# Dilated sliding-window attention, then a two-layer product: the first loads of w_in by columns, later landings in the order's list, longer zero matmuls, and new ranks

## The chip, the cores and the metric

The kernel runs on one core of a Trainium2 chip. The metric is the device time of one execution in microseconds. Before the change it is 316.99 us, the median of 4 runs (316.38 to 318.28).

## The reference

Attention of 8 batches with 8 heads, 576 positions and head size 64, under two masks: heads 0 to 3 see the last 32 positions, heads 4 to 7 every fourth of the last 128. Its output, with heads side by side, is the input x (4608 x 512) of two products with a leaky ReLU between them.

```python
scores = scale * np.matmul(q, k.transpose(0, 1, 3, 2))
mask_plain = (rel >= 0) & (rel < window)                                  # window = 32
mask_dil = (rel >= 0) & (rel < window * dilation) & (rel % dilation == 0)  # dilation = 4
attn = softmax(where(mask, scores, -1e9))
x = (attn @ v), transposed to (4608, 512)
h = x @ w_in                       # w_in is 512 x 2048
g = np.maximum(0.01 * h, h)
out = g @ w_out                    # w_out is 2048 x 512, all float32
```

## The kernel before

**Work.** Four pairs of batches make four blocks `m` of 1152 token columns, each cut into three chunks of 384. For a chunk, `up` (L776) makes 16 groups `j`, each of four matmuls that add up over the four 128-row blocks of w_in and give 128 of the 2048 hidden columns (the "products with w_in", L784); ACT applies the leaky ReLU (L791) into `gt`. `down` (L815) then makes three token tiles `tt`, each of four pieces `p` of four matmuls with w_out (the "products with w_out", L829); piece p needs the rows of w_out for j = 4p to 4p+3. DVE copies the sums out (L839) and SP stores them. The weights stay in SBUF in 16 bits.

**Attention.** `attend` (L878) goes through the head pairs in the order 2, 3, 0, 1: `load_group` loads q, k and v, `turn` transposes q and k (for the first two batches on TensorE, L555, with copies out of PSUM at L505 and L507), and `unit` (L636) makes scores (L664 adds the mask's bias for some batches, L667 and L683 the scores), exp on ACT (L689), a mask multiply on DVE (L703) where no bias was added, the products with v and with ones (L715 to L747), and the reciprocal of the sum as ln and exp on ACT (L759, L761). A multiply on DVE (L765) puts the normalized result into `xt`. The first two batches are done in two parts: part 0 covers positions below 384 or so and feeds chunks 0 and 1; part 1, the rest, feeds chunk 2 with data of its own (`load_rest`, L388).

**Loading the weights.** `load_w` (L419) loads w_in in eight eighths and w_out in eight, 512 KB each, into buffers that are still free, and casts each in two halves of 512 elements a partition. An eighth of w_in holds 512 columns of two of the four row blocks, so groups 0 to 3 need both eighths 0 and 1:

```python
            j0, i0 = n // 2 * 512, n % 2 * 2
            src = dram(moe_w_in, i0 * 128 * DFF + j0, [DFF, 128], [128 * DFF, 2], [1, 512])
            dst = [w_in[:, i * DFF + j0:i * DFF + j0 + 512] for i in (i0, i0 + 1)]
```

The casts of eighths 0 and 1, and those of w_out, go to POOL or DVE; those of eighths 2 to 7 of w_in to POOL alone.

**Order.** Nothing is scheduled by the compiler: every instruction is a task with an engine, a cost, dependencies and a rank, and `_Plan.run` (L83) makes one list. It goes forward in its own time and takes, on each engine, the ready task of the lowest rank. The engines then run their parts of that list strictly in order, whatever really becomes ready first. The plan estimates a load's landing from its issue, a shared server with a service time by packet size (`took`, L228), and an amount `LATE` that is added for loads after the opening; the loads of the opening get 0. The string `FIRST` (L19) gives the opening's loads their ranks from -1499 upwards: b and v are batch 0's q, k and v, i an eighth of w_in, o one of w_out, c and y batch 1's q, k and v, 0 and 1 the rests. `CON` is the rank of the load of the masks.

The ranks of compute tasks: chunk c's group j has `begins[c] + j * 1.3` (chunk 0 from 0, chunk 1 from 20.8), its product piece with w_out `begins[c + 1] + (tt * 4 + p) * 1.73 + 0.6`. The head pairs of batches 0 and 1 have `first + step * n` from `RANKS` (L20), in the order batch 0 part 0, batch 0 part 1, batch 1 part 0, batch 1 part 1; later batches have theirs from `WHEN`.

**Zero matmuls.** Where the plan leaves TensorE a gap ahead of the first product with w_out, the last loop fills it with matmuls of zeros (L919), 256 columns each, one for each 0.2 us of the gap (0.14 near the start).

Of the kernel before, what the change touches and what calls it, by code (L numbers as in the profile page):

```python
# [15 lines left out]
AHEAD, LATE = 5.0, 4.0  # L16
WHEN = (-5.0, 15.0, 50.0, 77.0, 112.0, 138.0, 172.0, 200.0)
CON = -1484.5
FIRST = "bvbviiii0iicooiicoyoooooy1"  # L19
RANKS = ((20.0, 6.0), (-40.0, 2.0), (20.0, 1.0), (40.0, 3.0))  # L20


def _constants():
# [36 lines left out]
class _Plan:  # L60
# [5 lines left out]
    def add(self, eng, dur, lat, deps, fn, prio, soft=0.0, kind=""):  # L66
        choices = eng if isinstance(eng, tuple) else ((eng, dur),)
        t = _Task(choices, lat, deps, fn, prio, soft, len(self.tasks), kind)
        self.tasks.append(t)
        return t  # L70
# [66 lines left out]
def kernel(  # L137
# [10 lines left out]
    nc = tc.nc  # L148
# [6 lines left out]
    DFF = moe_w_in.shape[1]  # L155
# [14 lines left out]
    def sbuf(name, shape, dt=FP16):  # L170
        return sb.tile(shape, dt, name=name)

    def bank(name, dt=FP32):
        return ps.tile([128, 512 if dt == FP32 else 1024], dt, name=name)

    def at(tl, p0, p1, off, *dims):

        row = tl.ap[0][0]
        return bass.AP(tensor=tl.tensor, offset=tl.offset + p0 * row + off,
                       ap=[[row, p1 - p0]] + [list(d) for d in dims])  # L180

    def dram(t, off, *dims):
        return bass.AP(tensor=t.tensor, offset=t.offset + off, ap=[list(d) for d in dims])
# [6 lines left out]
    w_in = sbuf("w_in", [128, NI * DFF])  # L190
# [21 lines left out]
    warm = sbuf("warm", [128, 512])  # L212
# [7 lines left out]
    fps = [bank(f"fps{i}") for i in range(2)]  # L220
# [7 lines left out]
    def took(n, size):  # L228
        for a, ta, b, tb in ((4, 9.0, 128, 15.0), (128, 15.0, 256, 19.0), (256, 19.0, 1024, 48.0),
                             (1024, 48.0, 2048, 85.0)):  # L230
            if size <= b:
                return n * (ta + (tb - ta) * (size - a) / (b - a)) / 16e3
        return n * size / 23.5 / 16e3

    def load(queue, dst, src, n, size, deps, prio):
        eng = ENG[queue]
        return plan.dma(queue, 0.7 if size == 128 else 0.48, took(n, size), deps,
                        lambda e: eng.dma_start(dst, src), prio,  # L238
                        LATE if prio > -1500 + len(FIRST) else 0.0)

    def cast(dst, src, n, deps, prio, engines=("POOL",)):
        cost = {"POOL": 0.05 + n * 0.00102, "DVE": 0.08 + n * 0.00056, "ACT": 0.06 + n * 0.00087}

        def fn(e):
            if e == "ACT":
                nc.scalar.copy(out=dst, in_=src)
            else:
                ENG[e].tensor_copy(out=dst, in_=src)  # L248
        return add(tuple((e, cost[e]) for e in engines), None, 0.2, deps, fn, prio, 0.0, "cast")
# [6 lines left out]
    def ring(name, n, users):  # L256
# [5 lines left out]

    t_warm = clear("POOL", warm.bitcast(FP32), 0.25, 0.0, -2000)
    t_id = load("ACT", con[:, 0:128], const_d[:, 0:128], 128, 256, [], -1498.95)
    t_bias = load("ACT", con[:, 128:128 + NMASK], const_d[:, 128:128 + NMASK], 128, 2 * NMASK, [],
                  -1498.5)
    t_con = load("SP", con[:, 128 + NMASK:NCON], const_d[:, 128 + NMASK:NCON], 128, 2 * NMASK, [],
                 CON)

# [13 lines left out]
    def clear_ones(slots, deps, prio=-700):  # L283
        for i in slots:
            t_ones["d", i] = clear("POOL", at(vd[i].bitcast(FP32), 0, 128, D // 2, [64, 16], [1, D // 2]),
                                   0.48, TWO_ONES, prio,
                                   deps)
            t_ones["p", i] = clear("POOL", at(vp[i].bitcast(FP32), 0, 128, D // 2, [64, 12], [1, D // 2]),
                                   0.38, TWO_ONES, prio,
                                   deps)  # L290
# [6 lines left out]
    CENG = ("POOL", "DVE")  # L297
# [121 lines left out]
    def load_w(n, prio):  # L419

        home, off, prev = w_home[n]
        f = home if home.dtype == FP32 else home.bitcast(FP32)
        st = f[:, off:off + 1024]
        users = w_used[n]
        old = w_used[prev] if prev is not None else []
        if n < 8:
            j0, i0 = n // 2 * 512, n % 2 * 2
            src = dram(moe_w_in, i0 * 128 * DFF + j0, [DFF, 128], [128 * DFF, 2], [1, 512])
            dst = [w_in[:, i * DFF + j0:i * DFF + j0 + 512] for i in (i0, i0 + 1)]
        else:  # L430
            j0 = 2 * (n - 8)
            src = dram(moe_w_out, j0 * 128 * DM, [DM, 128], [128 * DM, 2], [1, DM])
            dst = [w_out[:, j * DM:j * DM + DM] for j in (j0, j0 + 1)]
        t = load("SP", at(st, 0, 128, 0, [512, 2], [1, 512]), src, 256, 2048, old, prio)
        for i in range(2):
            c = cast(dst[i], st[:, i * 512:i * 512 + 512], 512, [t], prio, ("POOL",) if 2 <= n < 8 else CENG)
            users.append(c)
            if n < 8:
                for j in range(n // 2 * 4, n // 2 * 4 + 4):
                    w_in_t.setdefault(j, []).append(c)  # L440
            else:
                w_out_t[j0 + i] = [c]
# [417 lines left out]
    ranks = {}  # L860
    for n, step in enumerate(FIRST):
        seen = FIRST[:n].count(step)
        if step in "io":
            load_w(seen + (8 if step == "o" else 0), tick())
        elif step in "bvcy":
            ranks["bvcy".index(step) // 2, 1 - seen, step in "vy"] = tick()
        else:
            ranks[int(step)] = tick()
# [9 lines left out]
    def attend(b, part, first, step):  # L878
        units = {None: (0, 1, 2), 0: (0, 1), 1: (2,)}[part]
        if part == 1:  # L880
            load_rest(b, ranks[b])
        for n, hp in enumerate((2, 3, 0, 1)):
            if part != 1 and n % 2 == 0:
                load_group(b, hp // 2, *(ranks[b, hp // 2, i] if b < EARLY else tick()
                                         for i in (0, 1)))
            got = turn(b, hp, part or 0, first + step * n)
            for u in units:
                unit(b, hp, part or 0, u, got, first + step * n)

    n_c = 0  # L890
    for m in range(B // 2):
        for b in (2 * m, 2 * m + 1):
            if b < EARLY:
                attend(b, 0, *RANKS[2 * b])
                if b == 0:
                    release()
                    clear_slots(range(4, NT), -700, x_done[0, 0][-1:])
                    clear_ones((2,), x_done[0, 0][-1:])
                attend(b, 1, *RANKS[2 * b + 1])
            else:  # L900
# [14 lines left out]
    order = plan.run()  # L915


    def idle(e):
        nc.tensor.matmul(fps[0][:, 0:256], warm[:, 0:128], warm[:, 0:256], start=True, stop=True)  # L919

    pe = [t for t in order if t.eng == "PE"]
    for t, u in zip(pe, pe[1:]):
        if u.kind == "D":
            break
        x = t.start + t.dur + 0.1
        step = 0.14 if t.start < 8 else 0.2
        while t.start > 0.5 and x + step + 0.1 < u.start:
            w = _Task((("PE", step),), 0.0, [], idle, 0, 0.0, 0, "w")
            w.eng, w.start, w.dur, w.done = "PE", x, step, x + step
            order.append(w)  # L930
            x += step
# [37 lines left out]
```

## Time and profile before

| | |
|---|---|
| median of 4 runs | 316.99 us (316.38 to 318.28) |
| profiled execution | 317.19 us |
| its span, first to last instruction | 315.4 us |
| mean granted TensorE clock | 0.993 |
| TensorE busy | 303.0 us, 96% of the span |
| HBM read, written | 41.30 MB, 9.44 MB |
| PE waits for DVE (xt) before the second w_in product | 2.2 us, once |
| PE waits for ACT (exp) before L664 | 1.4 us, twice |
| the chain that ended last | 85% PE, 4% DVE, 4% DMA |

Durations come from one execution taken by the hardware profiler; times are microseconds from the span's start. PE is the matmul part of TensorE and PEld its weight loads, which overlap. Matmuls are pipelined, so a row's length includes a tail that the next row overlaps. A bracket at the end of a row says how long the engine stood idle before it and what ended the wait. POOL is GpSimd, DVE VectorE, ACT ScalarE, SP the engine that issues most of the DMAs. The page cuts the span into 40 slices of 7.9 us and gives each engine's busy share in tenths.

### The profile page before, as it was taken

What the parts mean: (1) busy time and instruction counts of PE and PEld (TensorE: products, weight loads), DVE (VectorE), ACT (ScalarE), POOL (GpSimd) and SP (SyncE); (2) the same over time, 40 slices, a digit from 0 to 9 for tenths busy, and PEclk for the clock granted to TensorE, in tenths of its full rate; (3) what the DMA queues carried; (4) which work ended last, traced back from release to release, by engine and by line L of the source; (5) the groups of instructions that cost most, each with busy time, mean ns of one, the idle gap of its engine ahead of it and who ended that gap; (6) DMA issues with size and microseconds to landing.
All of it is one profiled execution on the core that took longest, in us unless ns stands there. A gap on an engine that the chain in (4) does not pass through costs nothing.

```text
span 315.4 us, 6335 instructions
## 1 busy us (share of the span) xinstructions
PE 303.0 (96%) x2261; PEld 180.4 (57%) x2261; DVE 174.4 (55%) x394; ACT 219.8 (70%) x501; POOL 120.1 (38%) x176
## 2 busy tenths in 40 slices
PE   7869889999999999999999999999999999999995
PEld 3536545557776565666665555555555555555544
DVE  5845993725886978877659766664443421000011
ACT  3846773767889999999989888788787743334310
POOL 4458655365472755737447555370000000000000
PEclk9989999999999999999999999999999999999999
DMA  7999998999999999999989988711111111211113
GB/s 246 297 328 395 392 346 157 212 199 222 188 191 197 164 239 235 171 245 194 169 221 172 184 206 167 172 35 33 35 33 35 33 34 41 56 39 35 34 33 100
DMA packets 160223, 51.14 MB, mean 162 GB/s; under 512 B 139200, under 2 KB 151616, under 8 KB 160192
## 3 DMA queue, kind: packets, MB, share of 16 engines
q1 hardware_dynamic: 159744, 50.46, 67.5%
q8 instruction: 17, 0.28, 0.4%
q10 hardware_dynamic: 448, 0.29, 0.3%
q14 instruction: 14, 0.11, 0.1%
HBM read 41.30 MB, written 9.44 MB: 161 GB/s over the span
## 4 chain that ended last, share of the span: by engine, by line
PE 85%; DVE 4%; DMA 4%; SPq 2%; ACT 2%; issue 1%; DVEq 0%
PE fps L829 38%; PE hps L784 37%; PE sps L683 3%; PE ops L747 3%; SPq L238 2%; DMA gt<-in_moe_w_in_dram 2%; DMA stg<-in_k_dram 1%; DVE xt L765 1%; DVE slots L507 1%; DVE ee L703 1%; PE ops L737 1%; PE tp L555 1%; PE sps L667 1%; ACT rc L759 1%; ACT gt L791 1%
## 5 line engine op out<-in xcount | busy, mean ns | idle before, releaser
L784 PE MATMUL hps<-xt,w_in 128*128 128x384 f16 (+1 forms) x832 | 151.1, 316 | 2.4 <-DVE xt L765 2.2
L829 PE MATMUL fps<-w_out,gt 128*128 128x512 f16 (+1 forms) x592 | 145.0, 373 | 0.0
L791 ACT ACTIVATE gt<-hps 128x384 f16<-128x384 f32 (+1 forms) x208 | 94.2, 463 | 52.6 <-PE hps L784 49.4
L784 PEld LDWEIGHTS <-w_in 128*128 128x128 f16 x832 | 77.0, 98 | 47.3 <-issue 4.6
L829 PEld LDWEIGHTS <-gt 128*128 128x128 f16 x592 | 55.9, 98 | 45.8
L765 DVE TENSOR_TENSOR xt<-ops,rc 64x192 f16<-64x192 f32 (+2 forms) x138 | 52.0, 397 | 29.0 <-ACT rc L761 27.8
L703 DVE TENSOR_TENSOR ee<-ee,con 128x384 f16<-128x384 f16 x79 | 38.9, 496 | 33.9 <-ACT ee L689 33.1
L542 POOL COPY slots<-turned 64x576 f16<-64x576 f16 x48 | 34.6, 720 | 59.2 <-DVE turned L537 57.6
L839 DVE COPY osb<-fps 128x512 f32<-128x512 f32 (+1 forms) x37 | 24.7, 669 | 57.0 <-PE fps L829 56.6
L689 ACT ACTIVATE ee<-sps 128x384 f16<-128x384 f32 x92 | 44.8, 487 | 10.8 <-PE sps L683 9.5
L759 ACT ACTIVATE rc<-ops 64x384 f32<-64x384 f32 (+1 forms) x94 | 43.3, 463 | 11.5 <-PE ops L747 3.3
L761 ACT ACTIVATE rc<-rc 64x384 f32<-64x384 f32 (+1 forms) x96 | 46.6, 492 | 1.4
L248 POOL CAST nat<-stg 128x576 f16<-128x576 f32 (+1 forms) x53 | 35.5, 692 | 7.3 <-DMA stg<-in_q_dram 4.2
L683 PE MATMUL sps<-slots 128*128 128x192 f16 x152 | 25.0, 246 | 0.4 <-ACT ee L689 0.2
L683 PEld LDWEIGHTS <-slots 128*128 128x128 f16 x160 | 15.1, 102 | 12.0 <-issue 2.3
L548 DVE STREAM_TRANSPOSE slots<-nat 128x576 f16<-128x576 f16 x24 | 17.9, 761 | 2.8 <-POOL nat L248 2.8
L248 POOL CAST vd<-vst 128x1024 f16<-128x1024 f32 (+2 forms) x20 | 17.0, 872 | 5.7 <-DMA vst<-in_v_dram 5.0
L507 DVE COPY slots<-tp 64x128 f16<-64x128 f16 (+5 forms) x47 | 14.2, 319 | 7.7 <-PE tp L555 6.9
L537 DVE STREAM_TRANSPOSE turned<-nat 128x576 f16<-128x576 f16 x24 | 18.1, 764 | 0.2
L747 PEld LDWEIGHTS <-vp 128*128 128x128 f16 x160 | 11.1, 98 | 5.6 <-issue 0.2
L248 POOL CAST vp<-vst 128x768 f16<-128x768 f32 x16 | 13.1, 836 | 2.6 <-DMA vst<-in_v_dram 1.8
L747 PE MATMUL ops<-ee,vp 128*128 128x96 f16 x160 | 13.3, 206 | 0.0
(59 smaller groups left out, 125.3 us busy)
## 6 DMA issues: line engine op xcount, KB each, us to landing
vst<-in_v_dram SPq DMA_DIRECT2D x14, 512.0 KB, 5.0
stg<-in_q_dram SPq DMA_DIRECT2D x48, 144.0 KB, 3.7
stg<-in_k_dram SPq DMA_DIRECT2D x48, 144.0 KB, 3.0
vst<-in_v_dram SPq DMA_DIRECT2D x6, 768.0 KB, 5.7
out_dram<-osb SPq DMA_DIRECT2D x16, 192.0 KB, 2.3
gt<-in_moe_w_in_dram SPq DMA_DIRECT2D x5, 512.0 KB, 7.0
out_dram<-osb SPq DMA_DIRECT2D x24, 96.0 KB, 2.1
out_dram<-osb SPq DMA_DIRECT2D x14, 128.0 KB, 2.8
```

Source lines behind the costliest of these rows:

```text
L248: ENG[e].tensor_copy(out=dst, in_=src)
L542: lambda e, p0=p0, hh=hh: nc.gpsimd.tensor_copy(out=at(qb, p0, p0 + 64, hh * S + o, *od), in_=at(xb, p0, p0 + 64, i, *id_)), prio)
L683: nc.tensor.matmul(st[:, 192 * i:192 * i + 192], ka, qa, start=not by_pe, stop=i == 1 or not by_pe)
L689: lambda e: nc.scalar.activation(out=et, in_=st[:, 0:384], func=AF.Exp, scale=SCALE), prio + 0.1)
L703: ENG[e].tensor_tensor(out=io, in0=io, in1=mk, op=ALU.mult)
L747: nc.tensor.matmul(ot[:, c:c + 96], va, et[:, c:c + 96], start=True, stop=True)
L759: lambda e: nc.scalar.activation(out=r_out, in_=r_in, func=AF.Ln), prio + 0.2)
L761: lambda e: nc.scalar.activation(out=r_out, in_=r_out, func=AF.Exp, scale=-1.0),
L765: nc.vector.tensor_tensor(out=dst, in0=at(ot, p0, p1, c, *i_), in1=at(rt, p0, p1, c, *i_), op=ALU.mult)
L784: nc.tensor.matmul(ht[:, 0:n], w_in[:, i * DFF + j * 128:i * DFF + j * 128 + 128], at(xt[m % 2], 0, 128, i * 1152 + x0 + x, [1, n]), start ...
L791: lambda e: nc.scalar.activation(out=gt[c % NG][:, j * n_c + x:j * n_c + x + n], in_=ht[:, 0:n], func=AF.Prelu, alpha=0.01),
L829: nc.tensor.matmul(ft[:, 0:n_o], g[:, j * n_c + tt * 128:j * n_c + tt * 128 + 128], w_out[:, j * DM + c0:j * DM + c0 + n_o], start=(j == 0 ...
```

## The change

Four things change. Eighths 0 and 1 of w_in become 256 columns of all four row blocks, so eighth 0 alone serves groups 0 and 1, and eighth 1 groups 2 and 3. The plan counts loads of rank -1495 and above, up to the opening's end, as landing 0.8 us later; those are all loads of the opening after batch 0's q, k and v. Zero matmuls have 512 columns for each 0.3 us of a gap, or 256 for 0.2 at its end. Three pairs of `RANKS` change.

```diff
+AFTER = -1495.0
-RANKS = ((20.0, 6.0), (-40.0, 2.0), (20.0, 1.0), (40.0, 3.0))
+RANKS = ((20.0, 6.0), (-100.0, 2.0), (20.0, 2.0), (40.0, 4.0))
...
-                        LATE if prio > -1500 + len(FIRST) else 0.0)
+                        LATE if prio > -1500 + len(FIRST) else 0.8 if prio >= AFTER else 0.0)
...
-        if n < 8:
+        size = 512
+        if n < 2:
+            size, j0 = 256, 256 * n
+            src = dram(moe_w_in, j0, [DFF, 128], [128 * DFF, 4], [1, 256])
+            dst = [at(w_in, 0, 128, i * DFF + j0, [DFF, 2], [1, 256]) for i in (0, 2)]
+        elif n < 8:
...
-        t = load("SP", at(st, 0, 128, 0, [512, 2], [1, 512]), src, 256, 2048, old, prio)
+        t = load("SP", at(st, 0, 128, 0, [size, 1024 // size], [1, size]), src,
+                 128 * 1024 // size, 4 * size, old, prio)
...
-                for j in range(n // 2 * 4, n // 2 * 4 + 4):
+                for j in range(2 * n, 2 * n + 2) if n < 2 else range(n // 2 * 4, n // 2 * 4 + 4):
                     w_in_t.setdefault(j, []).append(c)
...
-        step = 0.14 if t.start < 8 else 0.2
-        while t.start > 0.5 and x + step + 0.1 < u.start:
-            w = _Task((("PE", step),), 0.0, [], idle, 0, 0.0, 0, "w")
+        while t.start > 0.5 and x + 0.3 < u.start:
+            n, step = (512, 0.3) if x + 0.4 < u.start else (256, 0.2)
+            w = _Task((("PE", step),), 0.0, [], idle(n), 0, 0.0, 0, "w")
```

More of the change, by code (lines that the diff above doesn't have):

```diff
@@ L433, in load_w @@
             dst = [w_out[:, j * DM:j * DM + DM] for j in (j0, j0 + 1)]
-        t = load("SP", at(st, 0, 128, 0, [512, 2], [1, 512]), src, 256, 2048, old, prio)
+        t = load("SP", at(st, 0, 128, 0, [size, 1024 // size], [1, size]), src,
+                 128 * 1024 // size, 4 * size, old, prio)
         for i in range(2):
-            c = cast(dst[i], st[:, i * 512:i * 512 + 512], 512, [t], prio, ("POOL",) if 2 <= n < 8 else CENG)
+            c = cast(dst[i], at(st, 0, 128, i * 512, [size, 512 // size], [1, size]), 512, [t], prio, ("POOL",) if 2 <= n < 8 else CENG)
             users.append(c)
             if n < 8:
-                for j in range(n // 2 * 4, n // 2 * 4 + 4):
+                for j in range(2 * n, 2 * n + 2) if n < 2 else range(n // 2 * 4, n // 2 * 4 + 4):
                     w_in_t.setdefault(j, []).append(c)
@@ L915, with idle @@
     order = plan.run()
-    def idle(e):
-        nc.tensor.matmul(fps[0][:, 0:256], warm[:, 0:128], warm[:, 0:256], start=True, stop=True)
+    def idle(n):
+        return lambda e: nc.tensor.matmul(fps[0][:, 0:n], warm[:, 0:128], warm[:, 0:n],
+                                          start=True, stop=True)
     pe = [t for t in order if t.eng == "PE"]
```

## The prediction

> **What bounds the kernel now.** I read the page first: busy shares, then the slices.
>
> ```profile
> PE 303.0 (96%) x2261; PEld 180.4 (57%) x2261; DVE 174.4 (55%) x394; ACT 219.8 (70%) x501; POOL 120.1 (38%) x176
> ...
> PE   7869889999999999999999999999999999999995
> ...
> PEclk9989999999999999999999999999999999999999
> DMA  7999998999999999999989988711111111211113
> ```
>
> A slice is 7.9 us. TensorE is full from the eighth slice to the last, so its work after about 55 us is a fixed block and only what it loses in the first six slices can move the end. The table of busy time by stretches confirms it: 60 to 80 us holds 20.00 us of PE, 110 to 200 holds 89.72. The waits of PE after 56 us sum to 0.4 us. The DMA row is the other limit: the engines are full from 8 to 46 us.
>
> Next the timeline from 14 to 34 us, where the first product with w_in starts.
>
> ```profile
> 16.67 0.43 DVE L248 CAST w_in<-gt 128x512 f16<-128x512 f32 x1 [1.05 <-DMA gt<-in_moe_w_in_dram]
> 16.70 0.87 POOL L248 CAST w_in<-gt 128x512 f16<-128x512 f32 x1 [1.69 <-DMA gt<-in_moe_w_in_dram]
> ...
> 17.02 0.35 DVE L765 TENSOR_TENSOR xt<-hps,rc 128x192 f16<-128x192 f32 x1
> 17.25 0.36 ACT L761 ACTIVATE rc<-rc 128x192 f32<-128x192 f32 x1
> ...
> 17.50 0.33 PE L784 MATMUL hps<-xt,w_in 128*128 128x384 f16 x1
> 19.02 0.43 DVE L248 CAST w_in<-gt 128x512 f16<-128x512 f32 x1 [1.66 <-DMA gt<-in_moe_w_in_dram]
> 19.05 0.87 POOL L248 CAST w_in<-gt 128x512 f16<-128x512 f32 x1 [1.48 <-DMA gt<-in_moe_w_in_dram]
> ...
> 19.36 0.61 DVE L765 TENSOR_TENSOR xt<-ops,rc 128x192 f16<-128x192 f32 x2
> 20.03 5.58 PE L784 MATMUL hps<-xt,w_in 128*128 128x384 f16 x23 [2.21 <-DVE xt L765]
> ...
> 22.41 1.17 POOL L248 CAST w_in<-wst 128x512 f16<-128x512 f32 x2 [0.21 <-DMA wst<-in_moe_w_in_dram]
> ```
>
> ACT had the last reciprocal at 17.61, but the two multiplies that finish xt stood on DVE behind a cast whose load landed only at 19.02. PE waited 2.21 us. Its clock then fell; the windows show it (columns: stretch, length, busy time of the five engines, granted clock, DMA share, GB/s):
>
> ```profile
> 21.20:24.20 3.00, 3.00 (x11) 1.39 (x10) 0.97 (x6) 0.99 (x3) 2.79 (x5) 0.50 1.06 353
> ...
> 24.40:25.00 0.60, 0.60 (x6) 0.34 (x5) 0.00 (x0) 0.33 (x1) 0.60 (x2) 1.00 1.06 362
> ```
>
> Half clock from 20.9 to 24.3 is 3.4 us, so 1.7 us of work is lost. The 23 matmuls took 5.58 us, against 23 x 0.163 = 3.75 at the full clock (a row of eight at 29.83 in the chain of waits takes 1.31). Wait and clock make 3.9 us, the largest sum in sight.
>
> The end of the opening, from the timeline of PE and POOL, decides how much of that is worth anything:
>
> ```profile
> 31.50 0.61 POOL L248 CAST w_out<-wst 128x512 f16<-128x512 f32 x1 [0.49 <-DMA wst<-in_moe_w_out_dram]
> ...
> 42.70 0.66 POOL L248 CAST w_out<-gt 128x512 f16<-128x512 f32 x1 [0.74 <-DMA gt<-in_moe_w_out_dram]
> ```
>
> ```profile
> 32.25 1.89 PE L829 MATMUL fps<-w_out,gt 128*128 128x512 f16 x8
> ...
> 41.33 0.32 PE L664 MATMUL sps<-con 128*128 128x384 f16 x1 [0.95 <-ACT ee L689]
> ```
>
> The casts of w_out wait for DMA one after the other (last one on DVE at 47.65 + 0.42), and the products with w_out follow them. Between 32 and 43 us PE waits 0.24 + 0.44 + 0.15 + 0.95 + 0.38 = 2.16 us in five places. Last, the chain of waits where chunk 1 begins:
>
> ```profile
> 55.64 0.46 DVE xt L765 x2
> ...
> 56.14 1.30 PE hps L784 x7
> ```
>
> Chunk 0's last product with w_out ends as batch 1's last xt appears. There is almost no stock of work there.
>
> **What the Trainium skill says.** "TensorE: Matmul & The Clock Gate", section "What's actually happening": the array falls to half clock after an idle window of about 3.4 us. The trace agrees in length (20.9 to 24.3). The same page, "Back-to-back issue gap", gives 512 columns about twice the time of 256; the trace has 1.73 us for 8, 0.216 each, and 0.94 less the tail for seven of 256 (about 0.11). "DMA: Bandwidth & Descriptors", "Why small descriptors are slow", gives each packet a fixed 3 cycles on top of 32 bytes a cycle: 1 KB instead of 2 KB is then 35/32 against 67/64, 4% more. The trace suggests more (below).
>
> **The change part by part.**
>
> *Column eighths.* Each of the two loads becomes 512 packets of 1 KB instead of 256 of 2 KB. The stretch 8 to 10 us, mostly 1 KB, moved 375 GB/s; 25 to 30, mostly 2 KB, 400. 524 KB cost 1.40 against 1.31 us, 0.09 more; against the 353 GB/s of 6 to 8 us, 0.17 more; the page's 4% is 0.05. I take 0.15 each, 0.3 for both (ends 0.1 and 0.4). DMA is full until 46 us, so every later landing of the opening moves by that. The four casts keep their 512 elements: 0.43 on DVE, 0.87 on POOL beside it. Gain: output groups 0 and 1 (8 matmuls, 1.30 us) need only the first load, cast by 16.70 + 0.87 + 0.15 = 17.7. The second cast ends at 19.05 + 0.87 + 0.3 = 20.2, after which groups 2 and 3 run to 21.5.
>
> *Loads counted later.* The list thinks that each load lands 0.8 us later, so on DVE the two multiplies come before the second cast: 17.61 + 0.35 = 18.0, or 18.4 with the first cast between. The first products start near 18.1 instead of 20.03 and end at 19.4. SP's order hardly moves: its issue slots are stretched (1.14 to 4.35 us) because the queue is full, and a load issued later by 1 us waits in a queue that takes 7 us to land anyway.
>
> *What is late next.* Groups 4 to 7 need the third and fourth eighths, unchanged halves by rows, which POOL casts until 22.41 + 1.17 = 23.6, now 23.9. The last two matmuls of group 4 and the four of group 5 then end at 24.7; before, the string of 23 ended at 25.45. Of 3.9 us only 0.7 arrives here. Then POOL is in the way (the fifth and sixth eighths end at 27.37, now 27.7), and at 32.4 the cast of the second eighth of w_out, 0.3 later than before. The 0.7 is spent by there, and the DMA price of 0.3 stays.
>
> *Longer zero matmuls.* 0.213 us in a step of 0.3 instead of 0.107 in 0.2: 71% of a planned gap against 53%. They run only where the list has a gap and end with the first product with w_out, so before 32.25. Cost: nothing where PE would wait; where data is early, at most one of them, 0.2 us. Gain: with PE busy from 18.1 the half-clock stretch should go. It is the gap 21.5 to 23.9 that could bring it back. I take zero for both; ends +0.8 (half clock from 24.3 on real work, 1.7 less about 0.9 of gaps and zero matmuls up to 32.4) and -0.2.
>
> *Ranks.* -40 to -100 has nothing between -100 and -34 to overtake, so nothing changes. Steps 1 to 2 put batch 1's four head pairs at 20, 22, 24, 26, where the first products with w_out have 21.4, 23.1, 24.9, 26.6: when both are ready, the products now go first. Steps 3 to 4 reorder batch 1's rest, where PE is full: nothing.
>
> *The list as a whole.* At 32.25 eight products went ahead of batch 1's first scores, and ACT idled 1.76 us before 34.70; its later exp then held PE up for 0.95 at 41.33. Products counted later should fall behind those scores. I take 0.9 off the 2.16 us; ends -2.1 (all gone) and +1.7 (two products of 0.86 more in the way).
>
> Sum: +0.3 - 0.9 = -0.6. Against the profiled execution, 317.19 (span 315.4 and 1.8 around it), 316.6; that execution lies 0.2 above the median of 316.99, so 316.4 on the median.
>
> **The rivals.**
>
> *A, no difference to speak of:* the sum above, 316.4, own range 315.4 to 317.6. For it: each later stage has a DMA or POOL wait of its own.
>
> *B, faster:* the 0.7 us passes on because batch 1's scores, not w_out, fill PE from 28 us, and all 2.16 us of waits go: -0.7 - 2.1 + 0.3 = -2.5, 314.5. For it: ACT idle 2.85 of 5 us at 30 to 35. Against: the masks land only at 33.2 and the last w_out at 47.
>
> *C, slower:* products overtake batch 1's last head pairs. The stock of products at 54 to 56 is used up early, and chunk 1 waits for the chain from the last values product (54.48) to xt (56.1). Two overtakings cost 1.7 us, plus 0.3 of DMA: +2.0, 319.0. It decides as soon as the last values product slips with fewer than one group of products (0.86 us) behind it. For it: the 0.04 us between xt and chunk 1. Against: both sides of the tie are gated by DMA until 48 us.
>
> *D, the DMA price alone:* the list's order stays as good as it was, 317.3.
>
> **How the numbers follow.** A 0.34, B 0.30, C 0.24, D 0.12. A difference of 0.5% (1.6 us) is about what a measurement tells from none: below 315.4 lies 0.28 of B and 0.05 of A, 0.33; above 318.6 lies 0.22 of C and 0.01 of A, 0.23; the rest 0.44. The range goes from 314.0, which cuts the far end of B, to 318.9, the middle of C.
>
> **What would show it.** Right: the first string of w_in products starts near 18.1 with no half clock behind it; the multiplies of xt stand before the second cast on DVE; group 5 ends near 24.7; the product at 32.25 starts no earlier than 32.2. Wrong: that product earlier by a microsecond; a half-clock stretch after 24.3; chunk 1 starting before 55 us (B) or after 57 with PE idle ahead of it (C).

## The result and the profile after

The changed kernel takes 318.40 us in the median of 36 runs (316.74 to 320.93), against 316.99 us for the kernel before, measured beside it (57 runs). The ratio is 1.0044, interval 1.0032 to 1.0056: slower by 0.44%, 1.4 us, small but clear of the noise. Forecast were 316.4 us and a small gain. The profiled execution took 318.98 us, its span is 317.2 us.

Each run is listed with its mean granted TensorE clock. One stretch of 3.4 us at half clock takes 1.7 of 317 us, so it shows as 0.995, two as about 0.99; "half-clock runs" below are those at 0.9955 or less, the others "full-clock runs". The changed kernel lists 37 runs, one more than its median counts.

From the page of the changed kernel: busy times, then slices of 7.9 us (PE, ACT, granted clock, DMA).

```profile
PE 305.1 (96%) x2253; PEld 179.2 (56%) x2253; DVE 172.1 (54%) x395; ACT 220.1 (69%) x501; POOL 119.3 (38%) x175
...
PE   8978979999999999999999999999999999999995
ACT  3845574666999999999988888788787843333310
PEclk9999999999999999999999999999999999999999
DMA  7999997989899999999999899811111111111113
```

The shape is that of before; in this execution the clock never fell. ACT is at 90% or more from the eleventh slice to the twentieth, some 80 to 160 us, which matters below.

The timeline of the changed kernel, opening (start, length, engine, line, operation; the last bracket is the idle time before and what ended it; lines are shifted by 7 against before, so the products with w_in are L791, those with w_out L836):

```profile
17.79 0.61 DVE L772 TENSOR_TENSOR xt<-ops,rc 128x192 f16<-128x192 f32 x2
17.93 0.34 PE L791 MATMUL hps<-xt,w_in 128*128 128x384 f16 x1 [0.24 <-DVE w_in L249]
18.45 2.69 PE L791 MATMUL hps<-xt,w_in 128*128 128x384 f16 x15 [0.19 <-DVE xt L772]
18.88 0.43 DVE L249 CAST w_in<-gt 128x512 f16<-128x512 f32 x1 [0.48 <-DMA gt<-in_moe_w_in_dram]
...
23.66 0.99 PE L791 MATMUL hps<-xt,w_in 128*128 128x384 f16 x5 [0.22 <-POOL w_in L249]
25.00 1.04 POOL L249 CAST rest<-stg 128x1024 f16<-128x1024 f32 x1 [1.39 <-DMA stg<-in_k_dram]
26.09 0.62 PE L562 MATMUL tp<-con,rest 128*128 128x128 f16 x8 [1.44 <-POOL rest L249]
...
32.77 1.38 PE L836 MATMUL fps<-w_out,gt 128*128 128x512 f16 x4
33.98 0.32 PE L671 MATMUL sps<-con 128*128 128x384 f16 x1
...
36.11 0.86 ACT L766 ACTIVATE rc<-ops 64x384 f32<-64x384 f32 x2 [2.65 <-PE ops L744]
41.74 0.49 ACT L696 ACTIVATE ee<-sps 128x384 f16<-128x384 f32 x1
42.28 0.32 PE L671 MATMUL sps<-con 128*128 128x384 f16 x1 [1.50 <-ACT ee L696]
...
57.63 1.30 PE L791 MATMUL hps<-xt,w_in 128*128 128x384 f16 x7 [0.26 <-DVE xt L772]
```

The two multiplies on DVE now stand ahead of the second cast (17.79 before 18.88), the string of sixteen starts at 17.93 and group 5 ends at 24.65. Then the early start is spent: the transposes of the rest wait 1.44 us for a cast that waits for a load, and the first product with w_out starts at 32.77, before at 32.25. Only four of those eight now stand ahead of batch 1's scores. But ACT idles 2.65 us there instead of 1.76, and the exp that TensorE needs later comes at 41.74: TensorE waits 1.50 us for it, before 0.95. Chunk 1 starts with a wait of 0.26 us.

So the parts do in the opening what they say, and neither this profile nor its clock says why the median is 1.4 us longer.

### The profile page after: what moved, and what is told of

It reads as the page before. It is cut to its first block, busy times and chain, and to the rows that moved or that the text cites. A ratio compares the mean times of both kernels' runs of the same rounds, so it can differ in the third digit from the quotient of the medians.

```text
span 317.2 us, 6321 instructions
## 1 busy us (share of the span) xinstructions
PE 305.1 (96%) x2253; PEld 179.2 (56%) x2253; DVE 172.1 (54%) x395; ACT 220.1 (69%) x501; POOL 119.3 (38%) x175
## 4 chain that ended last, share of the span: by engine, by line
PE 79%; DMA 7%; ACT 7%; SPq 3%; DVE 2%; issue 2%; DVEq 0%
PE fps L836 37%; PE hps L791 33%; DMA stg<-in_k_dram 4%; SPq L239 3%; PE sps L690 3%; PE ops L754 3%; DMA con<-consts 3%; ACT gt L798 2%; ACT rc L766 2%; ACT rc L768 1%; ACT ee L696 1%; PE ops L744 1%; DVE ee L710 1%; PE sps L674 1%; DVE slots L514 1%
## 5 line engine op out<-in xcount | busy, mean ns | idle before, releaser
L791 PE MATMUL hps<-xt,w_in 128*128 128x384 f16 (+1 forms) x832 | 150.7, 314 | 2.8 <-POOL w_in L249 1.6
L836 PE MATMUL fps<-w_out,gt 128*128 128x512 f16 (+1 forms) x592 | 145.4, 373 | 0.1
L791 PEld LDWEIGHTS <-w_in 128*128 128x128 f16 x832 | 76.2, 98 | 48.8 <-POOL w_in L249 3.4
L836 PEld LDWEIGHTS <-gt 128*128 128x128 f16 x592 | 55.8, 98 | 45.3 <-issue 0.4
L846 DVE COPY osb<-fps 128x512 f32<-128x512 f32 (+1 forms) x37 | 24.7, 670 | 56.1 <-PE fps L836 55.9
L710 DVE TENSOR_TENSOR ee<-ee,con 128x384 f16<-128x384 f16 x79 | 36.3, 463 | 28.0 <-ACT ee L696 27.1
L249 POOL CAST nat<-stg 128x576 f16<-128x576 f32 (+1 forms) x52 | 34.3, 683 | 9.2 <-DMA stg<-in_q_dram 3.5
L690 PEld LDWEIGHTS <-slots 128*128 128x128 f16 x160 | 15.2, 102 | 12.7 <-issue 2.6
```

What stands on the lines that cost most here:

```text
L690: nc.tensor.matmul(st[:, 192 * i:192 * i + 192], ka, qa, start=not by_pe, stop=i == 1 or not by_pe)
L710: ENG[e].tensor_tensor(out=io, in0=io, in1=mk, op=ALU.mult)
L791: nc.tensor.matmul(ht[:, 0:n], w_in[:, i * DFF + j * 128:i * DFF + j * 128 + 128], at(xt[m % 2], 0, 128, i * 1152 + x0 + x, [1, n]), start ...
L836: nc.tensor.matmul(ft[:, 0:n_o], g[:, j * n_c + tt * 128:j * n_c + tt * 128 + 128], w_out[:, j * DM + c0:j * DM + c0 + n_o], start=(j == 0 ...
```

## The experiments

Three sorts of cause were set against each other: the price of the DMA packets, the order of the work (in the opening, at chunk 1's start, or later on), and the clock. All runs in one view; "full" and "half" are the medians of full-clock and half-clock runs with their numbers:

```
kernel                       median us  before  ratio [95%]               full us (n)   half us (n)
changed                      318.40     316.99  1.0044 [1.0032, 1.0056]   317.93 (21)   319.27 (16)
e1  columns alone            316.73     316.89  1.0000 [0.9986, 1.0015]   316.73 (13)   317.11 (1)
e2  later counting alone     317.40     316.89  1.0020 [1.0008, 1.0032]   317.36 (20)   318.71 (2)
e3  zero matmuls alone       316.70     316.89  0.9995 [0.9982, 1.0009]   316.69 (13)   317.29 (1)
e4  ranks alone              317.62     316.89  1.0036 [1.0022, 1.0049]   317.52 (13)   318.24 (8)
e5  all but ranks            318.08     316.79  1.0049 [1.0032, 1.0066]   317.62 (11)   319.03 (9)
e6  all but later            317.55     316.79  1.0027 [1.0012, 1.0042]   317.44 (20)   319.00 (2)
e7  all but columns          318.15     316.79  1.0045 [1.0028, 1.0061]   317.94 (9)    319.12 (3)
e8  all but zeros            318.06     316.79  1.0041 [1.0026, 1.0057]   317.72 (15)   319.27 (7)
e9  changed opening          317.83     316.79  1.0027 [1.0010, 1.0043]   316.70 (11)   318.23 (11)
e10 changed middle           317.43     316.79  1.0018 [1.0007, 1.0030]   317.37 (16)   318.04 (6)
e11 two gaps filled          318.74     316.79  1.0059 [1.0039, 1.0080]   318.72 (3)    318.87 (4)
e12 columns and zeros        316.75     316.79  1.0011 [0.9996, 1.0026]   316.70 (11)   318.35 (3)
i1  exp wait filled too      317.54     316.54  1.0045 [1.0026, 1.0064]   317.54 (7)    none (0)
i2  early start, old order   316.85     316.54  1.0008 [0.9991, 1.0024]   316.68 (12)   318.35 (2)
```

The row of e5 leaves out one run of 322.42 us at a clock of 0.984. Of the kernel before's own 194 runs beside e1 to i2, 76 are half-clock runs, but they cost it only 0.1 to 0.5 us (beside e9 to e12, 19 of 52, medians 316.96 and 316.58).

A second view was worked out from the traces: the time at which a kernel's TensorE has streamed as many columns of real work (zero matmuls left out) as the kernel before, minus the time of the kernel before. This is its lag. Where a lag stays the same from one line to the next, nothing is lost between them. Up to 33 us TensorE has before's order in every kernel; between 34 and 44 us the orders differ in what they do first, and a lag read there rises and falls by more than a microsecond.

```
at us of before   changed  g1     g2     g3 (as e9)  e2     e4     e10    i1     i2
31                0.52     1.01  -1.18  -0.54       -1.26   2.13   0.29  -1.27  -1.63
33                0.87     1.04  -0.78  -0.18       -0.69   2.13   0.29  -0.88  -1.20
48                1.08     1.18  -0.54   0.07       -0.68   2.14   0.29  -0.64  -1.20
60                1.39     1.49  -0.22   0.39       -0.68   2.14   0.30  -0.33  -1.20
96                1.41     1.51  -0.21   0.39       -0.67   2.15   0.30  -0.32  -1.20
168               1.79     1.91   0.22   0.44        0.13   3.21   0.72   0.07  -1.19
304               1.79     1.91   0.22   0.44        0.13   3.21   0.72   0.07  -1.19
```

### The four parts alone: e1 to e4

Each is the kernel before with one part of the change's diff. e1 has the lines of `load_w` alone (the branch `n < 2` with its size, and the groups that it serves):

> The kernel before with only the first two eighths of w_in by columns. Theory L (landings: the 1 KB rows push every later load of the opening back, and all products behind them) expects most of the loss here, +0.8 to +1.5 us, and the masks' load to end the wait near 34.4 us as after the change instead of 33.2. Theory O (the list: loads counted later put casts, copies and scores in a worse order) expects -0.5 to +0.3. Theory C (clock: the half-clock stretch, harmless before because w_in was missing anyway, falls on real work) expects a first string of products with w_in near 18 to 18.5 us and, in the executions whose mean clock is below 0.996, about 1.2 us more than in the others.

e2 has `AFTER` and the 0.8 us alone:

> The kernel before with only the loads of the opening counted 0.8 us later. Theory O expects most of the loss here, +0.8 to +1.5 us; theory L expects 0 within 0.3, with the masks landing near 33.2 us; theory C expects the 2.2 us wait and the half clock gone or smaller, since the multiplies of xt no longer stand behind the second cast, though the products still need both eighths: 0 within 0.5.

e3 has the zero matmuls of 512 columns alone:

> The kernel before with only the longer zero matmuls. All three theories expect 0 within 0.3 us; theory C adds that the half-clock stretch at 21 us may go, which would then not shorten the time, since w_in is missing until 23.6 us.

e4 has the new `RANKS` alone:

> The kernel before with only the new ranks. Theory R (the rival of the prediction: products with w_out overtake batch 1's last head pairs and chunk 1 starves) expects +1 to +2 us with chunk 1's first product after 57 us; theories L, O and C expect 0 within 0.3 and chunk 1 near 56.1 us.

Columns and zero matmuls alone cost and bring nothing; they leave TensorE's and ACT's order of real work as it was. The DMA price is out: a 1 KB packet took 48.1 ns in the mean in the changed kernel, a 2 KB packet 90 there and 92 before, so two small ones cost some 4 to 6% more, under 0.1 us for a load, and by 45 us the bytes moved differ by 0.03 of 15.2 MB.

The later counting alone costs 0.20%, the ranks alone 0.36%. Both were expected to act in the opening, and neither does so. With the ranks alone every instruction up to about 62 us stands where it stood: in the kernel before's list -40 to -100 and the steps 1 to 2 each move nothing by themselves; the step 3 to 4 of batch 1's rest reorders about 180 of TensorE's 566 pieces of work between 62 and 204 us. e2 keeps TensorE's order up to 75 us and changes it after that. The lag of e4 is constant from 31 to 96 us and grows by 1.06 us between 96 and 168; that of e2 grows by 0.80. (e4's profiled execution began 2.1 us late, with two half-clock stretches, though its program is before's up to 62 us: so far do single openings differ.)

What happens there is seen in the timeline of e4, TensorE and ACT together, 128 to 137 us:

```profile
128.57 1.03 PE L829 MATMUL fps<-w_out,gt 128*128 128x512 f16 x4
...
129.60 1.03 PE L829 MATMUL fps<-w_out,gt 128*128 128x512 f16 x4
...
130.77 0.36 PE L683 MATMUL sps<-slots 128*128 128x192 f16 x2
130.96 1.03 PE L829 MATMUL fps<-w_out,gt 128*128 128x512 f16 x4
131.16 0.49 ACT L689 ACTIVATE ee<-sps 128x384 f16<-128x384 f32 x1 [0.45 <-PE sps L683]
...
132.19 0.49 ACT L759 ACTIVATE rc<-ops 64x384 f32<-64x384 f32 x1 [0.54 <-PE ops L747]
...
134.83 1.59 PE L784 MATMUL hps<-xt,w_in 128*128 128x384 f16 x8
136.64 0.33 PE L667 MATMUL sps<-slots 128*128 128x96 f16 x4 [0.22 <-ACT ee L689]
```

and of the kernel before in the same stretch:

```profile
128.25 1.03 PE L829 MATMUL fps<-w_out,gt 128*128 128x512 f16 x4
...
131.41 1.03 PE L829 MATMUL fps<-w_out,gt 128*128 128x512 f16 x4
...
133.95 1.03 PE L829 MATMUL fps<-w_out,gt 128*128 128x512 f16 x4
134.82 0.33 PE L667 MATMUL sps<-slots 128*128 128x96 f16 x4
...
137.44 1.03 PE L829 MATMUL fps<-w_out,gt 128*128 128x512 f16 x4
```

A piece of w_out needs no ACT; a group with w_in needs a leaky ReLU, a score an exp. Before, one piece of w_out stands between every few of the others. In e4 three stand in 3.4 us, ACT runs dry (0.45 and 0.54 us), and then groups that need ACT come close together and TensorE waits for it. ACT has no room to catch up. The row of stretches shows this for the kernel before (columns: stretch, length, busy time and count of PE, PEld, DVE, ACT, POOL, clock, DMA share, GB/s):

```profile
96.00:168.00 72.00, 71.58 (x574) 43.97 (x573) 54.32 (x112) 67.31 (x153) 39.13 (x54) 1.00 1.00 204
```

ACT is busy for 67.31 of 72 us. PE's busy column hides the loss, because a short wait for ACT falls into the modelled tail of the matmul before it. Summing the delays of single matmuls over 0.06 us from 96 to 170 us gives 0.74 us before, 1.16 in the changed kernel, 1.55 in e2, 1.79 in e4.

### All but one: e5 to e8

Each is the changed kernel with one part put back as before: e5 the ranks, e6 the later counting, e7 the columns, e8 the zero matmuls.

> The changed kernel with the ranks of before. Theory M (the list's order in the middle, 100 to 160 us, where ACT is nearly full, costs PE small waits for ACT; it is set by the ranks and by the later counting, and adds up part by part) expects 0.7 us less than the changed kernel's 318.4, so 317.7. Theory S (the opening: parts that are harmless alone cost about 1 us together, because batch 1's scores then stand behind late loads in PE's order) expects 316.7 to 317.2 if the ranks are one of them, with chunk 1's first product near 56 us, and 317.9 or more if they are not.

> The changed kernel with no load of the opening counted later. Theory M expects 0.5 us less than 318.4, so 317.9, with the middle's loss near that of the ranks alone. Theory S expects 317.4 or less, with chunk 1's first product near 56 us, since without the later counting PE's order in the opening is nearly that of before.

> The changed kernel with the first two eighths by rows as before. Theory M expects no difference from 318.4 within 0.3 us, as the columns alone made none. Theory S expects the same unless the columns are part of what costs in the opening (the early first string leaves PE idle at 25 us, and the half clock then falls on products that are needed): then 317.4 or less, and fewer executions with a mean clock below 0.996.

> The changed kernel with zero matmuls of 256 columns as before. Theories M and S expect 318.4 within 0.3 us. Theory C (the half clock on real work) expects 319 or more, with most executions below a mean clock of 0.996, since less of the gaps at 21 and 25 us is filled.

No part's removal gives all of the time back, so no single part is the cause; without the later counting (e6) it comes nearest, 1.0027 instead of 1.0044. The loss from 96 to 168 us is 1.02 us in e6, 1.62 in e7, 0.44 in e8, 0.38 in the changed kernel, but 0.01 in e5, which loses 1.05 between 48 and 60 us instead, where chunk 1 starts. So the price of an order can't be added up part by part. And e5 and e8 have many half-clock runs (9 of 20, 7 of 22), e6 two of 22. That is a second cost, apart from the order of the middle. (e6 lies between what the theories M and S expected; C's 319 us for e8 didn't come.) Columns and later counting together also change TensorE's order from 31 us on: the 4 and 4 of the timeline above. Neither does so alone, and e6 and e7, which lack one of the two, wait 0.81 and 0.83 us for the exp instead of 1.50.

### Opening and middle apart: e9, e10, e12

e9 is the changed kernel whose list is put back into the kernel before's order from 58 us of the list on; e10 has columns and zero matmuls only (opening in before's order) and the changed kernel's order from chunk 1 on. e12 is e10's control: columns and zero matmuls with before's order throughout. The edit (`LATER`, a long string that is left out here, names each piece of work and its engine in the order wanted):

```diff
     order = plan.run()
+    names = {"P": "PE", "A": "ACT", "D": "DVE", "G": "POOL", "S": "SP"}
+    later = {int(x[:-1]): (i, names[x[-1]]) for i, x in enumerate(LATER.split())}
+    for t in order:
+        if t.n in later:
+            t.start, t.eng = 1000.0 + later[t.n][0], later[t.n][1]
+    order.sort(key=lambda t: (t.start, t.n))
```

> The changed kernel up to chunk 1 (the list's time 58), and from there the order of the kernel before on every engine. Theory M (the loss sits in the middle's order) expects 317.0 to 317.3 us, most of the 1.6 us above the kernel before gone. Theory S (it sits in the opening: PE's order at 30 to 56 us, which only columns and later counting together change, and the half clock on products that are needed) expects 317.8 or more, with executions below a mean clock of 0.996 about 1.3 us above the rest.

> The kernel before with columns and zero matmuls (whose order of real work is that of before), and from chunk 1 on the order of the changed kernel on every engine. Theory M expects 317.8 us or more. Theory S expects 316.8 to 317.2, and the trace of the changed kernel (0.4 us lost between 100 and 160 us) says 317.2.

> The kernel before with columns and longer zero matmuls, without later counting and without ranks. The order of real work on PE and ACT is that of before. If the two parts add, 316.5 us (0.1 to 0.4 below the kernel before); it cannot tell faster from the same by more than that.

The opening alone gives 0.27%, the middle alone 0.18%; together 0.45%, beside 0.44% measured for the whole. The intervals are wide enough that this sum is no proof; the control e12 has 0.11%, with an interval that holds zero. The traces are clearer. e9's two (its own and g3) lose nothing between 96 and 168 us. e10 loses 0.42 us there, the changed kernel 0.38, e12 0.06: where this part is lost is settled. As theory S expected, e9 stays at 317.8 us with its half-clock runs far above the rest; e10's 317.43 us lies between S and M. e9 at full clock takes 316.70 us, some 0.1 more than before; most of its loss lies in the half-clock runs, 11 of 22, at 318.23.

### Zero matmuls into two waits: e11

```diff
+        for _ in range({5.2: 4, -100.0: 5}.get(u.prio, 0) if u.kind in ("", "U") else 0):
+            w = _Task((("PE", 0.2),), 0.0, [], idle(512), 0, 0.0, 0, "w")
```

> The changed kernel with four more zero matmuls ahead of group 4 (0.85 us) and five more ahead of the transposes of batch 0's rest (1.07 us), both in gaps where PE waited 1.0 and 1.44 us. If the half clock on needed products is a part of the loss (theory C), executions below a mean clock of 0.996 fall from 16 of 37 to under one in ten and the median falls by 0.3 to 0.6 us, to about 317.9; the median of the executions at full clock stays near 317.9. If the clock is no part of it, the median stays at 318.4 or grows by what the zeros delay.

The two waits for casts (21 to 23 and 24.7 to 26 us) get four and five more zero matmuls. It didn't help: 4 of 7 runs are half-clock runs, the median is 318.74. Either the clock had nothing to do with idle time, or the drop came from a wait that was left.

### Where the half clock falls: g1 to g4

g1 and g2 are the changed kernel again, g3 is e9, g4 is e5, each profiled in one more execution.

> Theory M (half clock on needed products): if this profile holds a window at half clock, it lies between 18 and 32 us, the w_in products in it take 2.6 to 2.8 us for eight where 1.46 is the rule, and the span is 318.0 to 319.0 us. Rival (the low-clock runs are long for another reason, later landings): the window lies in a wait for a cast between 21.5 and 26, where no product could run, and the span is as long all the same. At full clock neither is tested and the span is about 317.2 us.

> As for g1: the same kernel, a second look at where the half clock falls.

> The changed kernel's opening with the earlier order behind it. Theory M: with a half-clock window, it covers w_in products between 18 and 32 us and the execution takes about 318.2 us; without one, about 316.7 us and the lag behind the kernel before between 96 and 168 us is within 0.2 us of zero. Rival: window in a wait for a cast, and the time long all the same.

> All parts but the ranks. Theory M: with a half-clock window, it covers w_in products between 18 and 32 us and the execution takes about 319.2 us; without one about 317.6. Rival: window in a wait for a cast, and the time long all the same.

They took 319.10, 317.42, 317.63 and 318.93 us, the kernel before beside them 317.34. g1 and g4 caught it. The stretches of g1 (PE's busy time and count, clock, DMA share, GB/s):

```profile
21.20:24.62 3.42, 1.62 (x8) 1.00 1.06 324
24.62:28.04 3.42, 3.42 (x18) 0.50 1.08 391
```

and its timeline of PE:

```profile
24.25 1.46 PE L791 MATMUL hps<-xt,w_in 128*128 128x384 f16 x5 [0.22 <-POOL w_in L249]
25.50 1.06 PE L562 MATMUL tp<-con,rest 128*128 128x128 f16 x8
26.36 2.29 PE L791 MATMUL hps<-xt,w_in 128*128 128x384 f16 x8
```

At full clock (g2) these rows take 0.99, 0.62 and 1.46 us: 1.74 us lost, less the 0.69 us that g2 waits for the rest's cast at 24.40, so about 1.0 net. g1's casts were late too: the row that starts at 24.25 starts at 22.73 in g2, so g1's span of 317.3 us against g2's 315.6 isn't the clock alone. The expected 2.6 to 2.8 us for eight isn't met, as the window covers only most of them.

g4's window lies elsewhere, against the expectation. Its stretches:

```profile
38.43:41.85 3.42, 1.64 (x22) 1.00 1.05 399
41.85:45.27 3.42, 3.42 (x15) 0.51 1.14 340
```

and its timeline of PE:

```profile
40.33 0.32 PE L671 MATMUL sps<-con 128*128 128x384 f16 x1 [1.50 <-ACT ee L696]
...
41.72 1.72 PE L836 MATMUL fps<-w_out,gt 128*128 128x512 f16 x4
...
43.84 1.75 PE L836 MATMUL fps<-w_out,gt 128*128 128x512 f16 x4
```

Here the half clock falls on products with w_out (1.72 and 1.75 us where 1.03 is the rule), where TensorE had no wait to absorb it, right behind the 1.50 us for exp.

In all six traces with a drop the 3.42 us ahead of it were poorly filled: busy 1.21 us (before and e4), 1.58 (e12), 1.62 (g1), 1.64 (g4), 1.90 (e10). That is 35 to 56%, far from idle. The kernels with columns and later counting together (changed, e5, e8, e9, e11) share the wait of 1.50 us for exp; in before, e1, e2 and e3 it is 0.81 to 0.95.

Every trace records when the granted clock changes, and this shows what largely decides whether an execution drops. The clock first rises at 3.82 us in before, 4.14 in g1, 4.36 in g4, 4.84 in e12, 6.09 in e4 and 6.52 in e10. The drops come at 20.89, 24.62, 41.91, 25.32, 19.74 and 23.59: 5, 6, 11, 6, 4 and 5 times 3.413 us later. So each execution has a fixed row of windows of 3.413 us, which starts at another time in each. Count of each window only the time in which TensorE streams columns (0.213 us for 512, twice that at half clock, without the modelled tail of a matmul). In the 20 traces, with 1786 windows behind the first rise that have another one after them, the seven that are filled to 0.25 to 0.35 of what full clock could stream in them are each followed by one at half clock (in e4 two in a row). The emptiest of the others are filled to 0.40 (e7), 0.41 (e9) and 0.41 (g2), and no drop follows. How full the windows get depends on where they fall: a window of this length laid anywhere over g2, the changed kernel at full clock, reaches as little as 0.33 at two places, near 21 us and near 39 us, where the wait for exp is.

### The wait itself: i1 and i2

i1 is e11 with six more zero matmuls in the wait for exp, ahead of the score that follows it. They add zeros to a sum that is under way. i2 takes the wait away: before's order on all engines from the first product with w_out on, so that only the early multiplies and casts, columns and zero matmuls are left of the change.

```diff
+    def add(e):
+        nc.tensor.matmul(fps[0][:, 0:512], warm[:, 0:128], warm[:, 0:512], start=False, stop=False)
...
+    for _ in range(6):
+        w = _Task((("PE", 0.2),), 0.0, [], add, 0, 0.0, 0, "w")
```

> e11 (the changed kernel with its gaps before group 4 and before the transposes of the rests filled) and six more zero matmuls, adding zeros, in the 1.50 us for which TensorE waits for an exp near 40 us. Theory W (that wait is what the clock falls on): runs with a mean clock of 0.9955 or less fall from 4 of 7 in e11 and 43% in the changed kernel to under 15%, and the median comes down to about 317.7 us, the changed kernel's full-clock level of 317.9. Rival (the drops come from the casts' waits at 21 to 26 us or from something that zero matmuls don't touch): they stay at 35 to 55% and the median at 318.4 to 318.8 us.

> The changed kernel's columns, zero matmuls and early multiplies on VectorE, with the kernel before's order on every engine from the first product with w_out on, so that TensorE and ScalarE follow the order of before throughout. Theory W: the wait for exp is 0.8 to 1.0 us instead of 1.50, under 20% of the runs have the lower clock, and the median is 316.5 to 316.9 us, that is equal to the kernel before, and below e9's 317.83. Rival (the early start itself brings the drops): 40 to 50% of the runs have the lower clock and the median is 317.5 to 318.0 us.

The timeline of PE in i1, then in i2:

```profile
38.90 1.46 PE L930 MATMUL fps<-warm 128*128 128x512 f16 x6
40.56 0.32 PE L671 MATMUL sps<-con 128*128 128x384 f16 x1 [0.20 <-ACT ee L696]
```

```profile
17.36 2.93 PE L793 MATMUL hps<-xt,w_in 128*128 128x384 f16 x16
...
40.12 0.32 PE L673 MATMUL sps<-con 128*128 128x384 f16 x1 [0.81 <-ACT ee L698]
```

i1 has no half-clock run in 7, where the changed kernel has 16 of 37; at that rate none in seven would come in 2 of 100 cases. The traces, one execution each, say the same: a window laid anywhere over e11 between 10 and 66 us is filled under 0.375 only from 37.5 to 39 us on, at this wait; over i1 it is filled to 0.56 or more everywhere. So the drops that e11 kept come from this wait. The median fell to the changed kernel's full-clock level, as expected (317.54). But the kernel before was quicker beside it too, and the ratio, 1.0045 [1.0026, 1.0064], is no better than the changed kernel's. So the drops are not needed for the loss, and what they are worth in the median isn't resolved by seven runs.

i2 is as fast as before (1.0008), with 2 half-clock runs of 14. Its lag is constant from 33 us to the end, while that of i1, which starts about as early and has no drop either, grows by 0.95 us: 0.24 up to 48 us, 0.31 up to 60, 0.39 between 96 and 168. The zero matmuls fill i1's wait but don't bring the work behind it forward. The medians of the two, measured together, differ by 0.69 us, and the intervals of their ratios don't meet. i1 has 15 zero matmuls more than the changed kernel, which i2 lacks, but its lag grows where the order differs. So most of the loss comes from the order of the work from the first product with w_out on. Early start and old order together lose nothing, and gain nothing that these runs could tell.

## Why the prediction was wrong

**Right.** The columns' price ("0.3 for both") was nothing or some 0.1 us. The first string started at 17.93 (forecast 18.1), the multiplies went ahead of the second cast, group 5 ended at 24.65 (24.7), and "the 0.7 is spent by there": the product with w_out started at 32.77. In other profiled executions part of it lives on, 0.8 us ahead at 33 us in g2 and 1.2 in i2.

Three terms of the sum failed.

**The list as a whole, "I take 0.9 off the 2.16 us".** This is the largest miss. Products did fall behind the scores, by four, but the large waits of TensorE from 32 to 44 us are 0.34 + 1.50 + 0.29 = 2.13 us: none of the 0.9 came. The wait for exp grew from 0.95 to 1.50. Instead of gaining, the changed kernel falls back by 0.1 to 0.2 us between 33 and 48 us in its three traces, and by 0.3 more up to 60, where chunk 1 starts; e2 and i2, with before's order there, don't fall back at all. In its first profile chunk 1 starts at 57.63 behind a wait of 0.26 us, one of the signs of being wrong that the prediction named. That is the direction of rival C, at about a seventh of its 2.0 us, and through the order that columns and later counting make together rather than the ranks.

**Ranks, "Steps 3 to 4 reorder batch 1's rest, where PE is full: nothing."** With this fails "its work after about 55 us is a fixed block". PE is full there, but ACT is at 67.31 of 72 us, and the two are in step only through the order of their work. The steps 1 to 2, from which overtaking was expected, move nothing on the kernel before. The ranks alone cost 0.36%, and the trace shows it all between 96 and 168 us. In the changed kernel, whose list starts from other times, the same region loses 0.4 us.

**Half clock, "I take zero for both".** The skill's page "TensorE: Matmul & The Clock Gate", section "What's actually happening", speaks of an idle window; I looked for one and saw only the gap at 21.5 to 23.9. Here the measurement decides: windows filled to a third were enough. The page also says that the window runs freely, and the traces agree: the drops lie whole windows behind the first rise, and this rise comes at 3.82 to 6.93 us in the 20 traces. The kernel before has about as many half-clock runs (76 of 194), but in its profile the drop (20.9 to 24.3) covered products whose weights were late anyway, and these runs cost it 0.1 to 0.5 us. In the changed kernel they take 1.34 us more than the others, more than the end of +0.8 that was kept for them. As an estimate, 16 of 37 runs at 1.34 us against 76 of 194 at 0.4 make 0.4 us more in the mean.

**What stays open.** At full clock the changed kernel takes 317.93 us, the kernel before 316.5 to 316.6 in the groups beside e1 to i2, so some 1.4 less. The order of the work explains 0.9 of this in the traces (about 0.2, 0.3 and 0.4). e9, which shares the opening, takes only 0.1 more than before at full clock. The rest may be landings, which differ between executions of one kernel by more than a microsecond (the cast of the third eighth starts at 19.62 in g2 and at 21.05 in g1), or the machine's state from one group of runs to the next; no run separates it.

## What to carry to other kernels

TensorE at 99% doesn't make its order free: where the engine that feeds it is nine tenths busy, a piece of work that overtakes another moves waits into the full region, so compare the orders there whenever a rank or an estimate changes. Judge a half-clock stretch by what it covers; one that lies on a wait costs little, and moving work ahead of the wait can expose it. When filling gaps against the clock, find the emptiest stretches of about 3.4 us over the whole opening and not only the longest waits near the edit. When two orders are compared by the work done so far, read the lag where both have done the same pieces.

## What was not expected of the hardware

The clock fell to a half for 3.413 us at a time, after windows that were far from idle: filled to 0.25 to 0.35 with streaming columns, or busy for up to 1.90 of 3.42 us as the profile counts it (e10). Windows filled to 0.40 and more didn't bring it. A stretch as poor as 39% busy (22.20 to 25.62 us, 1.32 us) went by without a drop in the changed kernel's first profile, because no window lay on it: its clock first rose at 6.93 us, so its windows run from 20.58 to 24.00 and from 24.00 to 27.41, and these are busy for 2.15 and 1.97 us.
